# Thirty-two equal moving columns in the modulation products, two more dummy matmuls, and another arrangement of TensorE's branch

## The chip, the cores and the metric

The kernel runs on one core of one Trainium2 chip. The time is that of a whole execution on the device, in microseconds (us). Beside each time the execution's span is recorded (first to last instruction); it is usually 1.8 us shorter.

## The reference

A block with modulated layer norms: attention with 32 query heads on 8 cached key and value heads of which the last 512 positions count, then an MLP with a ReLU. The modulation comes from a small vector `c`.

```python
def reference(A_x, A_k_cache, A_v_cache, A_wq, A_wo, B_x, B_w1, B_w2, c, w_mod):
    x = A_x                                              # 1 x 2048 x 512
    mod = (_silu(c) @ w_mod).reshape(c.shape[0], 6, 1, -1)
    sa, ca, ga, sb, cb, gb = (mod[:, i].copy() for i in range(6))   # written out in the original
    h = _layernorm(x, axis=-1) * (1 + ca) + sa
    x = x + ga * _A_ref(h, A_k_cache, A_v_cache, A_wq, A_wo)        # attention and output projection
    h = _layernorm(x, axis=-1) * (1 + cb) + sb
    x = x + gb * _B_ref(h, B_w1, B_w2)                              # relu(h @ w1) @ w2, 512 -> 1792 -> 512
    return x
```

## The kernel before

The first modulation columns are made on TensorE: for each of 32 blocks of `w_mod` the block is the stationary operand and one column of silu(c) the moving one.

```python
    def mod_cols_mm(which, bk):
        ...
                    fs.append(lambda ...: mm(
                        bank[bk][:, col:col + 1], wm[sl][:, cc, c2 * P:(c2 + 1) * P], sc_bf[:, cc:cc + 1], ...))
```

`warm(n)` issues n dummy matmuls of 512 columns, whose results nobody reads. The start of TensorE's stream, in order:

```python
    warm(10)                 # while x, c and w_mod are on their way
    silu_exp(5)
    # ... layer norm of the first tiles, with warm(3) and warm(2) gated by it
    for f in fs: f()         # the 32 modulation products
    ln_tposes(0, TB[0])      # transposes of the normalised tiles
    mod_cols_evac(0, QBK)
    ln_tposes(1, TB[0])
    warm(2, bk=1)
    ln_tposes(2, TB[1])
    ln_tposes(3, TB[1])
    q_half(0, 0, CC_ORDER, QBK)   # first Q products, later s_half: first scores
```

The fast path assumes that the softmax needs no shift by its maximum. A flag says whether that was right, and every engine branches on it late in its stream: to the rest of the fast path, or to a long general kernel (`rerun`). The arm that is written first is reached by falling through, the other by a jump. For TensorE alone, before writes the fast path's last part first, so TensorE falls through in the MLP (90 ns in before's trace) and must jump over the rerun when it is done (3,850 ns).

```python
                if name == "pe":
                    with e.If(v == 128):
                        last_part()
                    with e.Else():
                        rerun()
                else:
                    with e.If(v != 128):
                        rerun()
                    with e.Else():
                        last_part()
```

## Time and profile before

| | before |
|---|---|
| time, median of six executions of two sessions | 560.22 us (559.86 to 560.32) |
| span of the profiled execution | 559.0 us |
| matmuls / TensorE's busy share | 4139 / 99% |
| TensorE's branch in the MLP / at the end of its part | 90 ns / 3,850 ns |
| from the last VectorE operation's start to SyncE's last branch | 2.41 us |

The DMA view of the last microseconds (553 to 560) gives the packets of the instruction queue, and for each of the last four outputs the time from issue to landing:

```profile
q8 instruction: 2, 0.03, 1.9%
issues: line engine op xcount, KB each, median us to landing
out_dram<-PT SPq DMA_DIRECT2D x1, 128.0 KB, 1.7
out_dram<-PT ACTq DMA_DIRECT2D x1, 64.0 KB, 3.0
out_dram<-PT SPq DMA_DIRECT2D x1, 32.0 KB, 2.6
out_dram<-PT ACTq DMA_DIRECT2D x1, 32.0 KB, 2.0
```

Two packets of 16,384 bytes are on the instruction queue q8 there (at 556.17 and 559.27). I call such a packet a page and its time on the queue a fetch. What I call the end runs from the last VectorE operation (timeline) to SyncE's last branch (view of its line, start to 0.1 us):

```profile
556.16 0.29 DVE L1754 TENSOR_TENSOR PT<-PT,x 128x128 bf16<-128x128 f32 x1
```
```profile
L1882 SPq COMPARE_BRANCH  x1: 43/43/43, 558.6 to 558.6; - x1
```

### The profile page before, as it was taken

Reading aid. Unit: us, or ns where it says so; the run is one execution under the profiler, and the core shown is the slowest. Engines: PE = TensorE matmul, PEld = TensorE weight load, DVE = VectorE, ACT = ScalarE, POOL = GpSimd, SP = SyncE. Lnnn points to the kernel's source line nnn. Section 1 sums busy time; section 2 is a strip of 40 time slices with the busy share of each in tenths; the row PEclk is TensorE's granted clock in tenths of the full one; section 3 lists DMA queues with packets and bytes.
Section 4 is the critical chain, followed back from the end, with each engine's and each line's share of the span. In section 5 each row is a group of like instructions: output and inputs, shape, how many; then the busy total and the mean of one; then the engine's idle time right before and its main releaser. Section 6 shows DMA issues by size and latency. Waiting matters only on the chain.

```text
span 559.0 us, 9759 instructions
## 1 busy us (share of the span) xinstructions
PE 553.9 (99%) x4139; PEld 316.6 (57%) x4139; DVE 254.9 (46%) x556; ACT 349.4 (63%) x455; POOL 52.7 (9%) x50
## 2 busy tenths in 40 slices
PE   8999999999999999999999999999999999999997
PEld 4665555555555555555555555555555554444444
DVE  5555555553546544335445443333354438322134
ACT  5986666666666666666666666666666644432500
POOL 2000022004400000033000000332000000000000
PEclk9999999999999999999999999999999999999999
DMA  9999763422224244353353312121123110200001
GB/s 234 296 196 185 136 166 42 114 43 73 38 41 74 39 84 106 61 130 58 96 95 57 76 40 39 39 38 38 39 39 76 39 29 0 50 28 21 21 29 48
DMA packets 113356, 42.66 MB, mean 76 GB/s; under 512 B 93976, under 2 KB 112152, under 8 KB 113304
## 3 DMA queue, kind: packets, MB, share of 16 engines
q1 hardware_dynamic: 112584, 41.08, 35.5%
q10 hardware_dynamic: 720, 0.89, 0.5%
q8 instruction: 33, 0.54, 0.4%
q14 instruction: 19, 0.16, 0.1%
HBM read 18.35 MB, written 2.10 MB: 37 GB/s over the span
## 4 chain that ended last, share of the span: by engine, by line
PE 98%; DMA 1%; SPq 0%; DVE 0%; issue 0%
PE psS L1374 29%; PE psO L1374 27%; PE psQ L1374 23%; PE psW L1374 20%; DMA wmw<-in_w_mod_dram 1%; SPq L1303 0%; PE psS L1377 0%; PE psO L1377 0%; DVE PT L1752 0%; DVE PT L1754 0%; PE psW L1377 0%
## 5 line engine op out<-in xcount | busy, mean ns | idle before, releaser
L1498 ACT ACTIVATE PT<-psS 128x1024 bf16<-128x1024 f32 x254 | 260.4, 1027 | 127.0 <-PE psS L1374 126.9
L1374 PE MATMUL psS<-qT,kT 128*128 128x512 bf16 (+1 forms) x516 | 151.8, 377 | 0.1
L1374 PEld LDWEIGHTS psO<-v,PT 128*128 128x128 bf16 x2048 | 126.6, 98 | 30.2
L1374 PE MATMUL psO<-v,PT 128*128 128x129 bf16 x2048 | 137.0, 220 | 0.0
L1374 PE MATMUL psW<-wo,oT 128*128 128x512 bf16 x512 | 130.6, 379 | 0.0
L1374 PE MATMUL psQ<-hT,wq 128*128 128x512 bf16 (+1 forms) x508 | 129.6, 377 | 0.0
L1508 DVE RECIPROCAL rinv<-psO 128x4 f32<-128x4 f32 x128 | 23.3, 182 | 225.3 <-PE psO L1374 225.3
L1509 DVE TENSOR_TENSOR o<-psO,rinv 128x512 bf16<-128x512 f32 x128 | 88.5, 691 | 4.7 <-DVE rinv L1508 0.3
L1374 PEld LDWEIGHTS psS<-qT,kT 128*128 128x128 bf16 x516 | 50.0, 98 | 58.7 <-issue 0.4
L1374 PEld LDWEIGHTS psQ<-hT,wq 128*128 128x128 bf16 x508 | 49.7, 98 | 59.0 <-ACT hT L1641 0.2
L1490 ACT ACTIVATE qT<-psQ 128x512 bf16<-128x512 f32 x125 | 73.9, 591 | 0.0
L1741 ACT ACTIVATE wq<-psS 128x512 bf16<-128x512 f32 x56 | 33.4, 597 | 49.1 <-PE psS L1374 49.1
L1374 PEld LDWEIGHTS psW<-wo,oT 128*128 128x128 bf16 x512 | 45.0, 98 | 32.9 <-DVE acc L1531 1.2
L1531 DVE TENSOR_TENSOR acc<-psW,acc 128x512 f32<-128x512 f32 x48 | 33.2, 691 | 6.7 <-PE psW L1374 6.7
L1374 PE MATMUL psO<-wmw,wq 128*128 128x512 bf16 (+1 forms) x168 | 32.9, 352 | 0.0
L1534 POOL TENSOR_TENSOR acc<-acc,gaf 128x512 f32<-128x512 f32 x12 | 15.6, 1301 | 146.9 <-DVE acc L1531 139.8
L1390 POOL TENSOR_TENSOR rstd<-rstd,cst 128x4 f32<-128x4 f32 x7 | 7.2, 1027 | 216.6 <-DVE rstd L1389 216.6
L1752 DVE TENSOR_TENSOR PT<-psO,gbf 128x512 f32<-128x512 f32 (+1 forms) x12 | 7.5, 624 | 40.4 <-PE psO L1374 40.4
L1374 PE MATMUL psS<-h2T,wmw 128*128 128x512 bf16 x112 | 25.3, 379 | 0.0
L1374 PEld LDWEIGHTS psO<-wmw,wq 128*128 128x128 bf16 x168 | 15.4, 98 | 16.5
L1374 PE MATMUL psS<-hT,wmw 128*128 128x512 bf16 x112 | 24.5, 379 | 0.0
L1384 DVE BATCH_NORM_STATS2 st<-x 128x6 f32<-128x512 bf16 x31 | 21.1, 680 | 3.7 <-DMA x<-in_A_x_dram 3.7
(93 smaller groups left out, 197.1 us busy)
## 6 DMA issues: line engine op xcount, KB each, us to landing
wo<-in_A_wo_dram SPq DMA_DIRECT2D x4, 1024.0 KB, 5.9
wq<-in_A_wq_dram SPq DMA_DIRECT2D x7, 512.0 KB, 4.5
wmw<-in_B_w_dram SPq DMA_DIRECT2D x14, 256.0 KB, 3.1
wmw<-in_w_mod_dram SPq DMA_DIRECT2D x4, 512.0 KB, 5.0
oT<-o SPq DMA_TRANSPOSE x128, 2.4
out_dram<-PT SPq DMA_DIRECT2D x15, 128.0 KB, 1.7
x<-in_A_x_dram SPq DMA_DIRECT2D x3, 512.0 KB, 4.3
v<-in_A_v_cache_dram SPq DMA_DIRECT2D x8, 128.0 KB, 4.5
```

Source lines behind the costliest of these rows:

```text
L1374: kb.op(PE, lambda e: e.matmul(out_ap, lhsT, rhs, start=start, stop=stop), reads=reads, group_writes=[R_b[k] for k in bk], signal=signal)
L1384: kb.op(DVE, lambda e: e.bn_stats(st[:, t, :], x_sb[:, t, :]), reads=[R_x[t]], writes=[R_st[t]])
L1390: kb.op(POOL, lambda e: e.tensor_tensor(rstd[:, sl], rstd[:, sl], cst[:, 0:1].to_broadcast([P, hi - lo]), op=ALU.pow), reads=R_rstd[sl] + ...
L1490: kb.op(ACT, lambda e: e.activation(qT[u % NQT][:, :], bank[bk], ACTF.Copy), reads=[R_b[bk]], writes=[R_qT[u % NQT]])
L1498: kb.op(ACT, lambda e: e.activation(PT[u % NPT][:, pr * 2:pr * 2 + 2, :], s_ps[pr][:, :, :], ACTF.Exp, scale=scale), reads=[R_b[pr * 2], R ...
L1508: kb.op(DVE, lambda e: e.reciprocal(rinv[:, u, :], o_ps[:, :, P]), reads=[R_b[5], R_b[6]], writes=[R_rinv])
L1509: kb.op(DVE, lambda e: e.tensor_tensor(o_sb[u % NOS][:, :, :], o_ps[:, :, 0:P], rinv[:, u, :].unsqueeze(2).to_broadcast([P, TPB, P]), op=A ...
L1531: kb.op(DVE, lambda e: e.tensor_tensor(acc[:, tl, :], bank[WBK], acc[:, tl, :], op=ALU.add), reads=[R_b[WBK], R_acc[tl]], writes=[R_acc[tl]])
L1534: kb.op(eng, lambda e: e.tensor_tensor(acc[:, tl, :], acc[:, tl, :], gaf[:, :], op=ALU.mult), reads=[R_acc[tl], R_ga], writes=[R_acc[tl]])
L1741: kb.op(ACT, lambda e: e.activation(h1T[b % 2][:, fc, :], bank[bk], ACTF.Relu), reads=[R_b[bk]], writes=[R_h1[b % 2][fc]], pre=all_events( ...
L1752: kb.op(DVE, lambda e: e.tensor_tensor(yt[i][:, c0:c1], bank[bk][:, c0:c1], gbf[:, c0:c1], op=ALU.mult), reads=[R_b[bk], R_gb], writes=[R_ ...
```

## The change

The intent, as far as the code tells it: give TensorE's array more to do in the thin stretch of the start (wider products, two more dummies), by my guess for the sake of its clock, which fell to half there in one of the runs below (e7, 7.83 to 11.25 us); and order the branch of TensorE as on the other engines, with the jump in the middle of the MLP, where matmuls are queued, instead of at the end.

```diff
+    NR = 32
...
-                        bank[bk][:, col:col + 1], wm[sl][:, cc, c2 * P:(c2 + 1) * P], sc_bf[:, cc:cc + 1],
+                        bank[bk][:, col * NR:(col + 1) * NR], wm[sl][:, cc, c2 * P:(c2 + 1) * P], sc_bf[:, cc:cc + 1].to_broadcast([P, NR]),
...
-        kb.op(DVE, lambda e: e.tensor_tensor(modc[:, mo:mo + 2 * DC], bank[bk][:, :2 * DC], m01[:, :], op=ALU.add), ...)
+        kb.op(DVE, lambda e: e.tensor_tensor(modc[:, mo:mo + 2 * DC], bank[bk][:, :2 * DC * NR].rearrange("p (c r) -> p c r", r=NR)[:, :, 0], m01[:, :], op=ALU.add), ...)
...
-    warm(2, bk=1)
+    warm(3, bk=1)
...
     ln_tposes(3, TB[1])
+    warm(1, bk=1)
...
-                def last_part():
-                    kb.emit(stream, e, n_ops)
-
-                def rerun():
+                with e.If(v != 128):
                     kb.emit(stream, e, n_ops)
                     ...                                  # the rerun, unchanged
-                if name == "pe":
-                    with e.If(v == 128):
-                        last_part()
-                    ...
+                with e.Else():
+                    kb.emit(stream, e, n_ops)
```

More of the change, by code (lines that the diff above doesn't have):

```diff
@@ L1439, in mod_cols_evac @@
         mo, r = which * 2 * DC, (R_moda, R_modb)[which]
-        kb.op(DVE, lambda e: e.tensor_tensor(modc[:, mo:mo + 2 * DC], bank[bk][:, :2 * DC], m01[:, :], op=ALU.add), reads=[R_b[bk], R_m01], writes=[r])
+        kb.op(DVE, lambda e: e.tensor_tensor(modc[:, mo:mo + 2 * DC], bank[bk][:, :2 * DC * NR].rearrange("p (c r) -> p c r", r=NR)[:, :, 0], m01[:, :], op=ALU.add), reads=[R_b[bk], R_m01], writes=[r])
     def mod_part(sl, cc):
@@ L1872, in rerun @@
                     gkb.emit(general[name], e)
-                if name == "pe":
-                    with e.If(v == 128):
-                        last_part()
-                    with e.Else():
-                        rerun()
-                else:
-                    with e.If(v != 128):
-                        rerun()
-                    with e.Else():
-                        last_part()
+                with e.Else():
+                    kb.emit(stream, e, n_ops)
             with nc.allow_non_contiguous_dma(reason="tiny c vector load in column layout, value rows of 256 bytes"):
```

## The prediction

> **What bounds the kernel now.** I read the page first, then the timeline of TensorE in the first 12 us, the chain of waits, and last the branch and drain records, which the page does not count as busy.
>
> Page, parts 1 and 4:
> ```profile
> PE 553.9 (99%) x4139; PEld 316.6 (57%) x4139; DVE 254.9 (46%) x556; ACT 349.4 (63%) x455; POOL 52.7 (9%) x50
> PE 98%; DMA 1%; SPq 0%; DVE 0%; issue 0%
> ```
> TensorE is busy 99% of the span and is 98% of the chain that ended last. So whatever keeps TensorE waiting is added to the end, and whatever another engine does there is hidden. The change touches only three short places: the start (7 to 12 us), the branch in the MLP (about 510 us) and the last 4 us.
>
> Start, timeline of TensorE (start, length, instruction):
> ```profile
> 8.87 0.35 PE L1374 MATMUL psQ<-sc_bf,wmw 128*128 128x1 bf16 x8 [0.21 <-DMA wmw<-in_w_mod_dram]
> 9.08 0.61 PE L1377 MATMUL psS<-ident,xn 128*128 128x128 bf16 x8
> 9.53 0.60 PE L1374 MATMUL psS<-ones 128*128 128x512 bf16 x2
> 9.96 0.27 PE L1377 MATMUL psO<-ident,xn 128*128 128x128 bf16 x2
> ...
> 10.40 0.68 PE L1374 MATMUL psQ<-hT,wq 128*128 128x256 bf16 x4
> 10.92 0.60 PE L1374 MATMUL psO<-hT,wq 128*128 128x256 bf16 x4
> 11.65 0.27 PE L1374 MATMUL psS<-qT,kT 128*128 128x256 bf16 x1
> ```
> The last eight modulation products wait for a DMA (w_mod lands at 8.82 us); then come transposes, the two dummies, transposes again, and the first Q products. The only wait of TensorE between 9 and 20 us that a delay could hide in is inside 10.40 to 11.10. There the fourth Q product starts at 10.80 instead of 10.73, because ScalarE's hT part ends at 10.75. After 11.65 the chain is TensorE and nothing else.
>
> The branch, views of the instructions of the two lines of If and of the block's end (min/median/max duration in ns, first and last start):
> ```profile
> L1875 PEldq COMPARE_BRANCH  x2: 90/1970/3850, 509.9 to 554.6; - x2
> ```
> ```profile
> L1886 PEldq DRAIN  x1: 68/68/68, 558.6 to 558.6; - x1
> L1886 SPq DRAIN  x1: 13/13/13, 558.7 to 558.7; - x1
> ```
> TensorE's branch in the MLP falls through and takes 90 ns at 509.9; the one at its end jumps over the rerun and takes 3,850 ns from 554.6. TensorE drains at 558.56, just before SyncE at 558.74: SyncE, not TensorE, closes the block. What TensorE's queue held when the first branch ran:
> ```profile
> 513.05 0.96 PEld L1374 LDWEIGHTS psQ<-wmw,wq 128*128 128x128 bf16 x5
> 513.26 1.03 PE L1374 MATMUL psQ<-wmw,wq 128*128 128x512 bf16 x4
> ```
> The first matmul after the branch (output psQ, the third tile of the second y block) starts at 513.26, with no gap before it. So the sequencer was 513.26 - 509.95 = 3.3 us ahead of the array.
>
> [...] Whether 32 columns cost the same no run has shown yet. [...] the dummies start 0.43 us apart up to 6.1 us and 0.22 us apart from 6.94; it has one transition to full clock, at 6.87 us, and none back before 559.8. [...] a 16,384-byte packet of the instruction queue at 556.17, 0.96 us long, inside the 3,850 ns branch. [...]
>
> **The change part by part.**
>
> (a) 32 columns. The 32 products stay 32 instructions. [...] Their last result comes some 13 ns later (estimate: 32 columns at the 54 ns per 128 of the transposes), but VectorE's modc (9.26 to 9.43) is not what the next step waits for: hT starts at 9.73, after the transposes. [...]
>
> (b) Two more dummies. A dummy of 512 columns takes 0.216 us at full clock (9.525 to 9.741). The first delays the transposes of tiles 2 and 3 by 0.22 us, the second delays the Q products by another 0.22. Q products now start at 10.405 + 0.43 = 10.84 and no longer wait for hT: the fourth starts at 10.84 + 3 x 0.108 = 11.16 instead of 10.80. Cost 0.36 us; ScalarE's qT copy (11.12) and the score products (11.65) follow it, and nothing after has slack: +0.36.
>
> (c) The far jump in the MLP. I take the duration of the same jump on the same engine, 3,850 ns: from 509.95 it ends at 513.80. At the end, TensorE's drain comes 0.11 us after its branch ended; with that, the first weight load is at 513.91, and a weight load and its matmul start 4 ns apart when the queue is empty (10.798 and 10.802). 513.91 - 513.26 = 0.65 us of standstill, all of it passed on, as all later work is TensorE's: +0.65. The other 3.3 us of the jump lie beside matmuls already queued.
>
> (d) No jump at the end. TensorE's drain would come at about 555.9 instead of 558.56, but SyncE closes the block, so this gives nothing by itself. What it gives is the DMA: the last three output transfers have 15 of their 16 landings at 556.74, 557.16 and 557.96, and the sixteenth at 558.16, 558.32 and 558.48[...]. The same pattern is in the MLP: the output that landed at 537.78 has its sixteenth at 538.95, with an instruction packet at 536.83; most others have it within 0.02 us. SyncE's last wait ended at 558.49. Without the fetch it ends near 557.98: -0.5.
>
> Sum: 0.02 + 0.36 + 0.65 - 0.50 = +0.53 us. 560.22 + 0.5 = 560.7.
>
> **The rivals.**
> First, the clock: the wider products and the dummies look meant to keep the array's activity up between 7.4 and 10.4 us[...]. Against it: the profiled execution never falls back and took 560.87 us, longer than all three timed ones (559.86 to 560.32), which are within 0.46 us of each other. There is nothing to win unless the timed runs differ from the profiled one. I give it 10%.
> Second, the jump in the MLP is hidden altogether: the queue may hold more than 3.3 us, or the fetch be quicker, since fetches of that size lasted 0.88 to 1.5 us, or GpSimd's way be typical (branch at 478.15, next instruction at 481.14, so 2.99 us). Then c is 0 to 0.1 and the time 560.1. Against it: the duration of TensorE's own jump is measured. For it: the branch record may contain waiting that is not the jump's. 25%.
> Third, the end gives nothing: a sequential page fetch falls in the last 2 us by chance[...]. Then d is 0 and the time is 561.2.
> Fourth, the dummies' 0.36 us vanish in a later wait of the start, for instance ScalarE's exponentials around 14 to 19 us. I find no stretch there in which TensorE idles in the chain for another reason, so 15%; time 560.4.
>
> **Range and chances.** The single terms are uncertain by about 0.1 (b), 0.4 (c) and 0.3 us (d), together about 0.5; the runs of before spread by 0.46. That gives 559.9 to 561.5 for 8 in 10. 2% is 11.2 us, twenty times the sum of the terms; no step of the change has that leverage, so within 2% has 0.98.
>
> **What would show it.** Right: the timeline shows three dummies at 9.5 and one before the Q products, the first Q products of the second pair and the scores about 0.36 us later (11.65 to about 12.0); a gap of TensorE of 0.4 to 0.9 us at about 514, where before had none; TensorE's drain at about 556; the sixteenth landing of the last output within 0.1 us of the fifteenth. The 32 products still 25 ns apart would prove (a). Wrong: a second clock transition in either kernel, products further apart than 25 ns, no gap at 514, or a late sixteenth landing with no instruction packet beside it. A difference over 2 us either way would mean that a thing I do not see here, most likely the clock, decides.

The sum came to +0.53 us, with 0.02 us for (a), 0.36 for (b), 0.65 for (c) and -0.50 for (d). Without (a) the three terms make +0.51 us. The -0.50 us of (d) is an estimate from the landings, 558.49 less 557.98 us.

## More of the kernel before

The timeline of TensorE around the branch in the MLP (start, length, instruction) has one stream of matmuls without a hole:

```profile
507.22 6.21 PE L1374 MATMUL psO<-wmw,wq 128*128 128x512 bf16 x28
513.26 2.97 PE L1374 MATMUL psQ<-wmw,wq 128*128 128x512 bf16 x13
```

## The result, and the profile after

| | before | after |
|---|---|---|
| time, median of six (range) | 560.22 us (559.86 to 560.32) | 560.41 us (560.19 to 560.95) |
| mean of six | 560.17 us | 560.49 us |
| ratio, 95% interval | | 1.0006 (0.9993 to 1.0019): the same |
| span of the profiled execution | 559.0 us | 558.6 us |

A ratio is the mean time of one kernel's runs over the mean of the other's in the same rounds, so it is not quite the ratio of the medians. The difference of the means is +0.32 us.

The page of after, parts 1 and 4: TensorE is still the bound. Fewer matmuls are listed than before because some of their records are missing in this trace; the weight loads (4141 against 4139) show the two dummies.

```profile
PE 549.8 (98%) x4066; PEld 316.4 (57%) x4141; DVE 255.1 (46%) x556; ACT 349.7 (63%) x455; POOL 52.8 (9%) x50
PE 97%; issue 1%; DVE 1%; DMA 1%
```

The timeline of TensorE at the start:

```profile
7.00 0.97 PE L1375 MATMUL psQ<-sc_bf,wmw 128*128 128x32 bf16 x32
8.32 0.72 PE L1378 MATMUL psS<-ident,xn 128*128 128x128 bf16 x8 [0.36 <-DVE xn L1396]
9.10 0.60 PE L1375 MATMUL psS<-ones 128*128 128x512 bf16 x2
...
9.98 0.38 PE L1375 MATMUL psS<-ones 128*128 128x512 bf16 x1
10.20 0.60 PE L1375 MATMUL psQ<-hT,wq 128*128 128x256 bf16 x4
10.63 0.60 PE L1375 MATMUL psO<-hT,wq 128*128 128x256 bf16 x4
11.36 0.60 PE L1375 MATMUL psS<-qT,kT 128*128 128x256 bf16 x4
```

In this execution `w_mod` had landed before 7.00, so all products run in one go and everything starts earlier. That is the luck of a DMA and not the change: before's products waited for it in three pieces, while those of e1 and e2 (one column) ran in one go too, and those of e4 (32 columns) in two. I therefore count from the last transpose of the second tile, which starts at 9.47 in before and 8.83 in after. The first score product follows it after 2.18 us in before (11.65) and after 2.54 us in after (11.36, with one record of the three dummies missing): **+0.36 us**.

The view of the line of the branch, then that of the line of the block's end (durations in ns, minimum, median and maximum; first and last start in us):

```profile
L1861 PEldq COMPARE_BRANCH  x1: 3723/3723/3723, 509.7 to 509.7; - x1
```
```profile
L1875 PEldq DRAIN  x1: 1195/1195/1195, 554.8 to 554.8; - x1
...
L1875 SPq DRAIN  x1: 13/13/13, 558.4 to 558.4; - x1
```

The long branch is now in the MLP. TensorE drains 3.7 us earlier than before (554.85 instead of 558.56), but SyncE still closes the block (558.43). The timeline of TensorE around the branch now has a hole, where before had none:

```profile
506.93 6.21 PE L1375 MATMUL psO<-wmw,wq 128*128 128x512 bf16 x27
513.45 2.76 PE L1375 MATMUL psQ<-wmw,wq 128*128 128x512 bf16 x12 [0.31 <-issue]
```

The 0.31 us is counted from the modelled end of the last matmul. From start to start the two matmuls beside the hole are 0.69 us apart, where their neighbours are 0.216 us apart, so the **standstill** is **0.47 us**. The bracket gives "issue" as what ended it: no engine and no transfer that the profile shows.

The DMA view of after between 553 and 560 us has no packet of an instruction queue, and the last three outputs land as quickly as the first:

```profile
out_dram<-PT SPq DMA_DIRECT2D x1, 128.0 KB, 1.7
out_dram<-PT ACTq DMA_DIRECT2D x1, 64.0 KB, 1.5
out_dram<-PT SPq DMA_DIRECT2D x1, 32.0 KB, 1.5
out_dram<-PT ACTq DMA_DIRECT2D x1, 32.0 KB, 1.5
```

The last VectorE operation and SyncE's last branch:

```profile
556.36 0.29 DVE L1756 TENSOR_TENSOR PT<-PT,x 128x128 bf16<-128x128 f32 x1
```
```profile
L1871 SPq COMPARE_BRANCH  x1: 43/43/43, 558.3 to 558.3; - x1
```

From the start of the one to the start of the other it is 1.90 us instead of 2.41: **-0.51 us**. Between the score product and the end, the rest of the stream is the same: from the first matmul after the branch to the last matmul it is 42.32 us in before and 42.33 in after.

The three differences add up to 0.36 + 0.47 - 0.51 = +0.32 us, and the means of the times differ by +0.32 us. That they agree to the last digit is chance: the six times of one kernel spread by 0.5 us or more, the 95% interval of the ratio is -0.4 to +1.1 us, and each term is read from one execution. The times alone show no difference; the terms are what the traces show. The profiled span of after is the shorter one only because of the earlier `w_mod`.

### The profile page after: what moved, and what is told of

Its sections match the earlier page's. It is cut to its first block, busy times and chain, and to the rows that moved or that the text cites. A ratio compares the mean times of both kernels' runs of the same rounds, so it can differ in the third digit from the quotient of the medians.

```text
span 558.6 us, 9687 instructions
## 1 busy us (share of the span) xinstructions
PE 549.8 (98%) x4066; PEld 316.4 (57%) x4141; DVE 255.1 (46%) x556; ACT 349.7 (63%) x455; POOL 52.8 (9%) x50
## 4 chain that ended last, share of the span: by engine, by line
PE 97%; issue 1%; DVE 1%; DMA 1%
PE psS L1375 29%; PE psO L1375 27%; PE psQ L1375 22%; PE psW L1375 19%; DMA x<-in_A_x_dram 1%; DVE st L1385 0%; PE psS L1378 0%; DVE mv L1386 0%; PE psO L1378 0%; DVE xn L1396 0%; DVE rstd L1594 0%; DVE PT L1754 0%; DVE PT L1756 0%; DVE tmp L1425 0%; DVE sc_bf L1426 0%
## 5 line engine op out<-in xcount | busy, mean ns | idle before, releaser
L1375 PE MATMUL psW<-wo,oT 128*128 128x512 bf16 x452 | 118.2, 379 | 3.1
```

The source lines that it names most:

```text
L1375: kb.op(PE, lambda e: e.matmul(out_ap, lhsT, rhs, start=start, stop=stop), reads=reads, group_writes=[R_b[k] for k in bk], signal=signal)
```

## The experiments

**The theory**: the time is the sum of these three terms, and each belongs to one part of the change: the dummies delay the first scores, the jump leaves TensorE standing for as long as the branch outlasts the matmuls that are queued, and the end gains because no instruction packet comes beside the last outputs. **The rivals**: the clock decides (the columns win something by keeping it); the jump is hidden or the standstill has another cause; the end's gain has nothing to do with the packet. Twelve kernels ran, each five times, in three sessions; before ran nine times in each. Its medians there were 560.11, 560.01 and 560.03 us. The differences below are of means against before of the same session. "Start" is the time from that last transpose to the first score in the profiled execution, "standstill" the hole in the MLP, "end" the time from the last VectorE operation to SyncE's last branch, "rest" the mean of the time less the span.

| kernel | time - before | ratio (95%) | start | standstill | end | rest |
|---|---|---|---|---|---|---|
| before | | | 2.18 | 0.00 | 2.41 | 1.83 |
| after | +0.32 | 1.0006 (0.9993 to 1.0019) | 2.54 | 0.47 | 1.90 | 1.82 |
| e3_cols | -0.03 | 1.0000 (0.9987 to 1.0014) | 2.18 | 0 | 2.28 | 1.85 |
| e2_dummies | +1.30 | 1.0021 (1.0008 to 1.0035) | 2.54 | 0 | 2.32 | 2.89 |
| e6_pad4 | +1.04 | 1.0019 (1.0006 to 1.0033) | 2.18 | 0 | 2.40 | 2.75 |
| e12_jump_pad4 | +0.49 | 1.0009 (0.9996 to 1.0023) | 2.18 | 0.41 | 1.89 | 1.86 |
| e1_jump | +0.06 | 1.0002 (0.9988 to 1.0016) | 2.18 | 0.17 | 1.89 | 1.85 |
| e4_hint | +0.64 | 1.0013 (0.9999 to 1.0026) | 2.54 | 0.13 | 1.90 | 1.76 |
| e5_hint_early | -0.03 | 1.0000 (0.9986 to 1.0013) | 2.18 | 0.00 | 1.89 | 1.74 |
| e9_best | +0.27 | 1.0006 (0.9993 to 1.0020) | 2.18 | 0 | 1.89 | 1.76 |
| e8_hint_end | +0.55 | 1.0010 (0.9997 to 1.0024) | 2.18 | 0 | 2.32 | 1.80 |
| e7_net0 | +1.96 | 1.0036 (1.0022 to 1.0049) | 3.55 | 0 | 2.40 | 1.88 |
| e11_net0_cols | +0.59 | 1.0012 (0.9998 to 1.0026) | 2.54 | 0 | 2.23 | 1.85 |
| e10_jump_dum10 | +3.00 | 1.0047 (1.0034 to 1.0061) | 5.50 | 0.65 | 2.25 | 1.81 |

### The columns alone

e3_cols is before with the 32 columns and nothing else of the change (the first three hunks of the diff: `NR`, the products, their evacuation).

> The kernel before with 32 equal columns in the modulation products alone. My theory (term a): products still 25 ns apart, time +0.02 us, which this measurement cannot tell from zero. [...]

The median is 560.10 us, the difference -0.03 us. The timeline of TensorE in this run:

```profile
7.44 0.95 PE L1375 MATMUL psQ<-sc_bf,wmw 128*128 128x32 bf16 x32
```

Thirty-two products of 32 columns last 0.95 us from the first start to the last end; they start 25 ns apart, like those of one column. The columns cost nothing, and in before's place they win nothing that these runs can show.

### The dummies alone, and a surprise after the span

e2_dummies is before with the two dummies:

```diff
-    warm(2, bk=1)
+    warm(3, bk=1)
...
     ln_tposes(3, TB[1])
+    warm(1, bk=1)
```

> The kernel before with the two more dummies alone. My theory (term b): Q products of the second pair, scores and all that follows 0.36 us later, time +0.36 us. Rival (a wait of the start takes them up, or the copies from ScalarE and VectorE set the pace): +0.0 to +0.1 us. The start of the scores against the start of the last transposes before shows it in the trace apart from when the DMA lands.

The median is 561.63 us, +1.30 us: about a microsecond more than the 0.36 us of the theory. The start shows exactly 2.54 us, so the term itself is there, and the mean span is 558.52 us against 558.30 for before, +0.22. The rest of the loss, 2.89 - 1.82 = 1.07 us, lies after the span, where the profile shows no instruction. What can two dummies at 9 us do there? They make TensorE's stream four instructions longer (each has a weight load). So I added four instructions where they cost nothing, in the first wait of the start (e6_pad4):

```diff
     warm(10)
+    for i in range(2):
+        mm(bank[7][:, 0:1], ones[:, :], ones[:, 0:1], True, True, [R_ones], [7], i == 1)
     silu_exp(5)
```

> The kernel before with two one-column matmuls more in the first wait of TensorE (5 us), where they cost nothing: the program of TensorE is longer by four instructions, as with the two dummies. Theory 1 (the 1.2 us that the run with the dummies alone took after the end of its last recorded instruction[...]): time about 1 us above before, 3.0 us instead of 1.8 between the span and the time of the profiled execution. Theory 2 (they come from the dummies' work itself or from chance): same as before.

The median is 561.10 us, +1.04 us, with the start as in before, the mean span 558.32 us against 558.18, and the rest again 2.75 us instead of 1.85, between 2.29 and 3.14 in its five executions. So the microsecond goes with the four instructions ahead and not with what they do. If it depends on the jump at the end too, it must go when that jump goes. e12_jump_pad4 has the same four instructions, and the branch as in after:

> The branch part of the change with the four padding instructions of the padding run. Theory: the 1 us that the padding cost came after a far jump at the end[...]; without that jump it is gone: same as the branch part alone (560.0 to 560.4), 1.8 us after the span. Rival (the padding costs in itself, or wherever its end lies): about 561 again.

The rest is 1.86 us, so the microsecond is gone. The median is 560.27 us; the mean difference of +0.49 us hangs on one execution of 561.71 us with a span of 559.8, whose cause I don't know. Without it the four others are 0.2 us above before. Shown is thus: with the jump at the end, four instructions cost about a microsecond after the span, and without the jump they don't. That it is the fetch of a page behind the jump is not shown. A second page on q8, after the one during the jump, is fetched near 559 us in e2 and e6, but in before, e3, e7 and e11 too (559.27, 558.78, 560.16 and 558.75 us), and these four don't pay. The trace of e2 has one more packet than theirs, of 8 KB on the other instruction queue (q14), at 561.55 us, 1.19 us after the packet that is the last in theirs; the trace of e6 has none. What the microsecond is spent on stays open.

### The branch alone

e1_jump is before with the last hunk of the diff, the branch part.

> The kernel before with the branch part of the change alone (TensorE jumps far in the MLP, not at its end). My theory (terms c and d): a standstill of TensorE of 0.4 to 0.65 us after the branch in the MLP, SyncE's last wait some 0.5 us earlier after the last matmul[...]; the two nearly cancel, so the time is within 0.2 us of before. Rival 1 (the jump in the MLP is hidden): no standstill, 0.5 us faster. Rival 2 (the end gives nothing): standstill stays, 0.5 us slower.

The median is 560.00 us, +0.06 us. The end has its gain, 1.89 us against 2.41, and the standstill is there but small, 0.17 us. The view of the branch's line shows a shorter branch than in after:

```profile
L1860 PEldq COMPARE_BRANCH  x1: 3423/3423/3423, 509.5 to 509.5; - x1
```

The terms of e1 add up to 0.17 - 0.52 = -0.35 us, but its times are 0.06 us above before's on average (95% interval -0.7 to +0.9 us). So the gain of the end is seen in the trace and not in the time. Part of the gap may lie in the profiled execution of before, which took 560.87 us, longer than any of its timed ones: its end of 2.41 us is the longest of the six traces with the jump at the end (2.23 to 2.41), so that the gain is 0.34 to 0.51 us; and a standstill is known from one execution of each kernel only.

The standstill is, in each of five runs, the branch's duration less 3.25 us, which is what TensorE had queued. And the branch's duration follows the page that is fetched during it (16,384 bytes on the instruction queue; read from the packets of the packed traces). I take that page for the jump's target, which no packet says:

| run | fetch starts after the branch | fetch lasts | branch | branch less both | standstill |
|---|---|---|---|---|---|
| e4_hint | 0.99 us | 0.99 us | 3.38 us | 1.40 us | 0.13 us |
| e1_jump | 1.00 | 1.13 | 3.42 | 1.30 | 0.17 |
| e12_jump_pad4 | 0.98 | 1.33 | 3.66 | 1.35 | 0.41 |
| after | 0.98 | 1.34 | 3.72 | 1.40 | 0.47 |
| e10_jump_dum10 | 1.59 | 1.00 | 3.91 | 1.31 | 0.65 |
| before, jump at the end | 1.52 | 0.96 | 3.85 | 1.37 | |

### A hint that the branch will be taken

The language has a hint for a branch: a mark somewhere ahead of it. What it does on the chip, these runs had to show. e4_hint is after with such a mark 24 matmuls ahead; it needs the branch written out with labels.

```diff
-                kb.emit(stream, e, 0, n_ops)
+                if name == "pe":
+                    kb.emit(stream, e, 0, n_ops - HINT_OPS)        # HINT_OPS = 24
+                    hl = e.mark_branch_hint_location()
+                    kb.emit(stream, e, n_ops - HINT_OPS, n_ops)
...
+                    e.br_cond(v == 128, "pe_last_part", "pe_rerun").branch_hint(hl)
```

> The changed kernel with its branch of TensorE announced 24 matmuls ahead by a prefetch hint, nothing else changed. My theory (the standstill in the MLP is the instruction fetch of the jump's target): the branch of TensorE drops from 3.7 us to well under 1 us, the standstill of 0.47 us goes, the end keeps its gain: some 0.45 us faster than the changed kernel, 0.2 to 0.3 us faster than before. Rival (the standstill is the branch's own cost[...]): branch and standstill stay as they are. Third way: the hint does not take[...]: same as the changed kernel.

It failed as an experiment: the mark was passed at 504.44 us, but a page was fetched at 510.75, a microsecond after the branch, as without it. The branch took 3,379 ns. Away from the jumps, 207 to 282 records of TensorE lie between two page fetches in before's trace, and no fetch fell between the mark and the branch. So I tried a mark with such a fetch behind it: e5_hint_early puts it 170 matmuls ahead (passed at 473.72 us; a page is fetched at 481.04), on before with the branch part alone, the arms ending in a common label:

```diff
+HINT_OPS = 170
```

> Only the branch part of the change, with the prefetch hint 170 matmuls (about 35 us) ahead of TensorE's branch in the MLP instead of 24, so that it stands before the instruction fetch at 481 us. Theory: [...]no page was fetched between the late hint (504 us) and the branch (510 us) in the run with the late hint; so with the early one the branch takes well under 1 us, no instruction packet follows within 2 us of it, no standstill is left, and the end keeps its 0.5 us: 0.4 to 0.5 us faster than before. Rival (the hint has no effect on TensorE at all): branch 3.4 to 3.7 us and standstill 0.1 to 0.5 us as in the run of the branch part alone, time as there.

The view of the branch's line, then of the block's end:

```profile
L1882 PEldq COMPARE_BRANCH  x1: 385/385/385, 509.5 to 509.5; - x1
```
```profile
L1897 SPq DRAIN  x1: 68/68/68, 558.0 to 558.0; - x1
```

The same far jump takes 385 ns, TensorE doesn't stand still at all, and the end keeps its gain. So the standstill goes with the long branch, the one with a page fetched during it (3.38 to 3.91 us in the five runs above). Two things are not shown: that the mark had the target's page fetched ahead, and whether it worked for the fetch at 481.04 us or for standing 36 us ahead of the branch instead of 5. One thing was expected otherwise: a page packet still follows 1.09 us after the branch (510.57 us). The branch is over by then, and in e1, after and e4 too a packet comes 0.7 us after the branch's end, as here; so I take it for the page after the target, though a packet doesn't say which page it brings. Yet the median is 559.91 us, the difference -0.03 us: the half microsecond of the end does not come through whole. SyncE's drain comes 0.435 us after its last branch, and lasts 68 ns, where in after and e1 it comes after 0.174 us and lasts 13. Is that a detour through the common label? e9_best lets both arms go straight to the block's end:

```diff
-                        e.br("pe_joined")
+                        e.br(block.end_bb)
```

> The branch part with the early prefetch hint as before, but both arms of TensorE's branch go straight to the block's end, without the extra empty block that the two earlier builds with hints had. There, SyncE drained 0.43 us after its last branch instead of 0.17 us, which took back 0.26 to 0.3 us. Theory: with the drain back at 0.17 us the time is 0.3 to 0.5 us below before (the end's gain, no standstill). Rival (the later drain comes from the hint or from TensorE's new branch itself): 0.43 us again, and the time equals before within 0.1 us.

The drain still comes 0.435 us after SyncE's last branch, so the label is not it. The median is 560.03 us. Four executions are within 559.86 to 560.12 and one is 561.67 us; that one has a recorded mean clock of 0.997 instead of 1.0 and a span of 559.9 us instead of 558.1 to 558.4. It is told again below. No version beats before clear of the noise, and why SyncE drains later in the builds with a written-out branch stays open.

### The end

e8_hint_end leaves the fall-through in the MLP as in before and gives the hint to the jump at the end, with its mark at the start of the last part. If the gain of the end comes from the jump's being short, it must show here; if it comes from there being no page in it, it depends on whether one is left.

```diff
+                    with nc.body("pe_last_part", valid_engines=only):
+                        hl = e.mark_branch_hint_location()
                         last_part()
+                        e.br("pe_joined").branch_hint(hl)
```

> The kernel before with a prefetch hint at the beginning of TensorE's last part for the jump at its end. Theory[...]: no instruction packet between 554 and 558 us, TensorE's jump below 1 us, the last output's sixteenth landing within 0.1 us of its fifteenth, 0.5 us faster than before, with no standstill in the MLP. Rival (no effect of hints on TensorE): jump 3.5 to 3.9 us, sixteenth landing late, same as before.

The view of the jump's line, and the DMA view from 553 to 560 us:

```profile
L1880 PEldq COMPARE_BRANCH  x1: 347/347/347, 554.2 to 554.2; - x1
```
```profile
q8 instruction: 1, 0.02, 0.9%
...
out_dram<-PT ACTq DMA_DIRECT2D x1, 64.0 KB, 2.9
out_dram<-PT SPq DMA_DIRECT2D x1, 32.0 KB, 2.5
out_dram<-PT ACTq DMA_DIRECT2D x1, 32.0 KB, 1.9
```

The jump is short, 347 ns, but against the expectation a page is still fetched, at 555.63 us (1.1 us after the jump's end, so I take it for the one after the target), and the outputs land as late as in before. The end takes 2.32 us. The time is 560.57 us, +0.55 us, in which the late drain of SyncE is contained. So a short jump of TensorE did not shorten the end; a page was fetched in it, as in before (2.41 us). With pages there, the sixteenth landing of before's last three outputs comes 1.42, 1.16 and 0.52 us after the fifteenth (558.16, 558.32 and 558.48 us), in after, without a page, 0.00 to 0.03 us. That the page holds up one of the transfer's sixteen parts is how I read this; the traces don't tell on which DMA engine a packet lies.

### The clock

e7_net0 takes two dummies from the first ten and has the two of the change, so that the number of instructions is before's:

```diff
-    warm(10)
+    warm(8)
...
-    warm(2, bk=1)
+    warm(3, bk=1)
...
+    warm(1, bk=1)
```

> The two more dummies of the change with two of the ten first dummies taken out, so that the program of TensorE is as long as before. Theory: the 1.2 us after the span are gone (1.8 us again), the 0.36 us on the way to the scores stay: 0.3 to 0.4 us above before; first scores 2.54 us after the last transpose of tile 1, as in the run with the dummies alone. If the 1.2 us stay, the length of the program is not their cause. [...]

The rest is back to 1.88 us, which fits e6: with before's number of instructions the microsecond is not there. But the median is 561.90 us, +1.96 us. The windows view of this run, with its limits at the changes of the clock's record (length, then busy time of PE, PEld, DVE, ACT and POOL, the granted clock, the DMA share and GB/s):

```profile
4.42:7.83 3.41, 2.36 (x24) 0.92 (x24) 3.00 (x10) 2.06 (x8) 1.22 (x2) 1.00 1.31 331
7.83:11.25 3.42, 3.13 (x38) 2.44 (x37) 2.05 (x7) 1.83 (x3) 0.83 (x3) 0.50 1.03 212
```

The clock was released at 4.42 us (the record starts there), and halved again from 7.83 to 11.25. The start took 3.55 us. This is the first rival's case, seen for the first time. Would the 32 columns have held the clock? e11_net0_cols is e7 with the columns added, and again nothing else.

> The run with eight first dummies and two more later, now with 32 columns in the modulation products. That run lost 1.4 to 2.9 us because TensorE's clock fell back to half from 7.83 to 11.25 us. Theory A[...]: no fall in the profile, most executions at before + 0.4 us. Theory B[...]: executions as slow as in that run, 561.3 to 563.

The windows view of e11, from the start of its own clock record at 5.27 us, in stretches as long as e7's:

```profile
5.27:8.68 3.41, 2.75 (x41) 1.48 (x41) 3.17 (x14) 2.14 (x9) 1.95 (x4) 1.00 1.15 267
8.68:12.09 3.41, 3.23 (x32) 2.35 (x31) 2.24 (x8) 2.91 (x7) 0.10 (x1) 1.00 1.18 289
```

The clock stays, the start takes 2.54 us, and the median is 560.59 us: 1.3 us less than e7, with the five executions of e11 (560.40 to 560.97) all below the five of e7 (561.31 to 563.03, in another session; against before of each session it is 1.4 us less). (Its +0.59 us against before is 0.2 more than the dummies' 0.36, and e4's +0.64 is as little explained by its terms; sums of one execution's terms and means of five agree to some 0.3 or 0.4 us, not better.) So by the times of these two runs the columns are worth something beside eight first dummies. The two traces don't show that it was the columns that held the clock. In e7 and in e10 below, the clock fell 3.41 us after its release, and the array had been busy for 2.36 and 2.67 us of these. In e11 it was busy for 2.75 us of the 3.41 us from the release, and the clock stayed. But with products of one column it stayed too, with 2.72 us in e2 (4.12 to 7.53 us) and 2.81 in before (6.87 to 10.28); in the nine traces that have a clock record and no fall it was 2.72 us or more. Whether busy time is what counts, and where a limit would lie, no run shows. The release comes at another time in each execution (between 4.12 and 7.15 us in the eleven traces that have a record; after, e1 and e12 have none), 4.42 us in e7 and 5.27 in e11; that this saved e11 is a rival that no run excludes. How e7 loses is seen, in the trace or from the mean clock, for two of its executions only, the two with a mean clock of 0.997. That figure is what 3.42 us at half clock, as in e7's trace, make of a 560 us span (estimate: 1 - 0.5 x 3.42/560). The three others have 1.0 and are longer than e11's all the same, with spans of 559.4 to 561.1 us. A later release might do that and leave the figure at 1.0 (in before the dummies start 0.43 us apart up to 6.56 us and 0.22 us from 6.94, the record starts at 6.87 us, and the figure is 1.0), but no record of those executions shows it.

e10_jump_dum10 is e1 with ten more dummies instead of two, as a scale for the dummies' cost:

```diff
-    warm(2, bk=1)
+    warm(7, bk=1)
...
+    warm(5, bk=1)
```

> The branch part of the change with ten dummies more instead of two (five at each of the two places). Theory (every dummy past the first 0.07 us lies on the way to the end): first scores 10 x 0.216 - 0.07 = 2.1 us later after the last transpose of tile 1 (4.3 us instead of 2.18), time 2.1 us above the run of the branch part alone. Rival (later waits take dummies up): clearly less than 2 us. No jump at the end, so no cost after the span: 1.8 us.

The five times are 564.6 (the profiled one), 562.3, 562.79, 562.69 and 562.98 us. The profiled one fell to half clock, as this line of its windows view shows (its limits are again the record's):

```profile
8.61:12.03 3.42, 3.20 (x21) 1.93 (x23) 1.26 (x5) 1.39 (x3) 0.12 (x1) 0.50 1.04 240
```

Its start of 5.50 us therefore says nothing on the scale. The other four lie 2.6 us above before's mean on average and 2.5 above e1's; ten dummies, of which 0.08 us vanish in a wait as in after, would make 10 x 0.216 - 0.08 = 2.1 us. The profiled execution had besides a standstill 0.48 us longer than e1's and an end 0.36 us longer (2.25 against 1.89), which would make 2.9 us; whether the other four had these, no trace says. So 2.1 to 2.9 us hold what was measured, but this is no precise scale.

## Why the prediction was right

The stated range, 559.9 to 561.5 us, holds before's own 560.22 us as well, so the time alone confirms little. What confirms the steps is their terms in the traces, each seen again in a kernel that has that part alone.

**(a) The columns, +0.02 us in the sum: nothing to lose.** They start 25 ns apart (e3, after) and change the time by -0.03 us (e3), within the noise. The term took 23 to 25 ns for the spacing in before, a slip of reading. Before's trace has 25 to 26 ns within a piece, so that the term should have been 0.

**(b) The dummies, +0.36 us: right, and by the steps given.** Each delays by 0.216 us, and 0.08 us of the sum is taken back because the Q products no longer wait for ScalarE's hT part: in after the Q products run from 10.20 to the scores at 11.36 in 1.16 us, in before from 10.40 to 11.65 in 1.25. The start grew by 0.36 us in all four kernels that have the two dummies and the full clock (after, e2, e4, e11) and in none of those without. The fourth rival, a later wait that swallows them, fails: the stretch from the first score to the first matmul after the branch is 501.61 us in before, in e2 and in e5, and longer in after only by its standstill.

**(c) The standstill, +0.65 us: the reckoning is right, the term was mis-sized.** It measured 0.47 us in after and 0.17, 0.13 and 0.41 in the others of that branch. The failing piece is the duration taken over from the jump at the end, 3,850 ns: that jump's fetch started 1.52 us after the branch, most of those in the MLP start after 0.98 to 1.00, and the fetch itself lasts 0.99 to 1.34 us. And 3,850 ns was one sample: in the six traces with the jump at the end it took 3,510 (e11) to 3,850 ns. A slip of reading adds a little: TensorE's drain came 0.06 us after its branch had ended (558.50 to 558.56), not 0.11, which makes the estimate 0.60. The lead of 3.3 us was right (3.25), as was the conclusion that only what exceeds it counts: the branch less the standstill is 3.25 or 3.26 us in all five runs. In the one run whose fetch started late, e10, the standstill was 0.65. The second rival, a hidden jump, is nearly true for the executions with a quick fetch. With the early mark it is true outright (e5: 385 ns, no standstill).

**(d) The end, -0.50 us: right.** The end shrank by 0.51 us (0.34 to 0.51 with the other traces that have the jump at the end), the instruction packet is gone from it, and in e8 the end stays at 2.32 us with a packet in it and a jump of 347 ns. That the packet holds up a DMA engine was not shown. The third rival, a chance fetch in the last 2 us, did not come in after: its last 16 KB page was fetched at 530.70. It did come in e10, with its ten dummies: a page was fetched from 558.97 to 560.42, the output that had 15 landings at 560.78 had its sixteenth at 561.96, and the end took 2.25 us although TensorE jumps nowhere there.

**The first rival, the clock: not realised, but real.** No execution of before in these sessions has it: 27 of them have 0.999 or 1.0 as the mean clock, and none is above 560.5 us. With the 1-column products and the ten first dummies it did fall in two executions of the others, both with a mean clock of 0.997: e10's profiled one, and the slow one of e9, whose span was 1.65 us above the mean of its four others (half of the 3.42 us at half clock in e7 and e10 is 1.71 us, an estimate). In the 21 executions with 32 columns (after, e3, e4, e11) the mean clock never shows it. Two in some 70 against none in 21 doesn't prove an insurance; the times of e7 against e11 make it likely.

**What cancelled.** The intended gain of the branch, up to half a microsecond, is seen at the end of every trace without a page fetch there (1.89 or 1.90 us against 2.41); it does not come out of the noise in the times of e1, e5 and e9. The dummies cost 0.36 us in each of the four traces, against a fall of the clock that the mean clock of none of before's 27 executions shows, and the standstill (0.47 us in after) takes back most of the rest. The surprise of e2, a microsecond for the dummies without the new branch, is not part of the change's own result, as after has no jump at the end.

## What to carry to other kernels

Here a far jump cost a queued engine only what exceeded its queue (branches of 3.38 to 3.91 us with 3.25 us of matmuls queued: 0.13 to 0.65 us), so try it where long operations are queued. Try the language's mark well ahead of it too: 170 matmuls ahead, with a page fetch between, the branch took 385 ns and the standstill was gone; 24 ahead, with none between, it took 3,379 ns; and no version became faster clear of the noise. Look at a jump at the end of a program beyond its own engine: with a page fetched in it the end took 2.23 to 2.41 us here, without one 1.89 or 1.90. Dummy matmuls on the path cost nearly their full length each time (two of 0.216 us cost 0.36), so try equal moving columns first, in products that start no further apart for them (here 25 ns with 1 column or 32); and when a change of a few instructions moves the time by a microsecond (four instructions: +1.04 us in e6), look at the time less the span (2.75 us there instead of 1.85) before you explain it by the work.
